# Sharing the last four evictions, waiting for the last stores ahead of a branch, and later branch hints

## The chip, the cores and the metric

The kernel runs on one core of a Trainium2 chip. The core has TensorE (PE, matrix products into PSUM), VectorE (DVE), ScalarE (ACT), GpSimd (POOL) and SyncE (SP, which mainly issues DMAs). The metric is the device time of one execution in microseconds (us); lower is better.

## The reference

Two attention blocks on inputs of 2048 rows and 512 columns, 32 heads of 16 columns each, in bfloat16. Block A is linear attention, block B full softmax attention; their outputs lie side by side in one output of 2048 x 1024:

```python
# A: phi(t) = where(t > 0, t + 1, exp(t)) + 1e-6
kv  = einsum("bhsd,bhse->bhde", phi(k), v);  z = sum of phi(k) over the rows
a   = (phi(q) @ kv) / (phi(q) . z + 1e-6)        # heads side by side, then @ A_wo
# B: scores = q k^T * 16**-0.5 for each head, 2048 x 2048
b   = softmax(scores) @ v                        # heads side by side, then @ B_wo
out = concatenate([a, b], axis=-1)
```

## The kernel before

Block B is the bulk: 32 heads with 2048 x 2048 scores each. It is cut into 32 units (4 groups of heads, 4 stretches of 512 query rows, 2 head parities). TensorE makes blocks of scores in PSUM; ScalarE takes the exponential of most of them (line 1111), and VectorE with GpSimd makes the rest by an integer approximation (lines 988 and 1184). TensorE then multiplies the results with V into `pPV` (line 1245). Block A, the projections and the output products fill the gaps.

The order of the work on each engine is not written by hand. When the program is built, a planner in Python runs a model of the engines: each job is a list of stages with an engine and an assumed duration; a stage becomes a candidate when the one before is over and visible, and the planner always takes the candidate that could start first, priorities breaking near ties. `go` adds an assumed extra delay `JM` (0.8 us) after a stage on GpSimd. What the planner emits is kept per engine in program order (`Sched.add`); semaphore waits follow from reads and writes.

The last unit is split in two halves of 256 query rows (`last_half`). Each half is transposed out of PSUM (line 1309), its row sums inverted (1310), multiplied (1311, the first half on GpSimd, the second on VectorE), and transposed into `ON` (1313). The output product has four parts for each of the last four tiles of 128 rows. Three need only earlier heads, and run ahead into free PSUM banks (`ahead_cand`); the fourth, in `last_tiles`, needs `ON`: tiles 0 and 1 the first half, tiles 2 and 3 the second. Each tile is then evicted from PSUM (the copy is at line 548) and stored (line 1333), 128 KB a store, by the SyncE queue or, for tile 3, by ScalarE's.

The integer approximation holds for a bounded range only. So the kernel tests the row sums: `bound_job` (lines 631 to 645), then `flag_job`, a small matrix product (652) and a reduction into `FLG` (653). At the end of its program each engine waits for the flag, loads it into a register (1606), and branches (1609): if the flag is set, it runs a second, general softmax program; if not, as with these inputs, it branches over that program to a drain and the end of the block (315). GpSimd alone waits for all stores ahead of its branch, in the operation named `final`.

The general program is thousands of instructions long on TensorE, ScalarE and VectorE, so the target of their branch is far from the code that runs ahead of it. The code comes in by DMA as the program runs (the queues of kind "instruction"). A `BRANCH_PREFETCH_HINT` (line 1608) names a branch to come as likely taken. `emit_queue` places it a given number of operations (`mark[0]`) ahead of the end of an engine's program; one operation of TensorE can be several matmuls.

Of the kernel before, what the change touches and what calls it, by code (L numbers as in the profile page):

```python
# [247 lines left out]
def bass_concat_heads__linear_attn_block__softmax_full_mha__prompt_kernel(nc, A_x, A_wqkv, A_wo, B_x, B_wqkv, B_wo, out):  # L248
# [39 lines left out]
    JM = 0.8  # L288
    DSH = 0.45
    XNT = 0.63  # L290
    VVT = 0.69
    HINT = 60
    HQ = ("pe", "act", "dve")
    FW = 3.4
    UT = 0.6
    AE = 40.0
# [18 lines left out]
    with es:  # L315
# [57 lines left out]
        def f32v(bk, n=512):  # L373
            return bk[0][:, bk[2]:bk[2] + n]
# [73 lines left out]
        for e_ in range(2):  # L448
            sch.add("dve", lambda e, e_=e_: e.tensor_reduce(PAR[:, e_:e_ + 1], ZMk[:].rearrange("p (a e) -> p e a", e=2)[:, e_, :],
                                                           axis=AX.X, op=ALU.max),  # L450
                    reads=["ZMk"], writes=[("PAR", e_)])
# [17 lines left out]
        def vis(eng, en_):  # L469
            return en_ + TAIL[eng] + SEM  # L470
# [3 lines left out]
        def lease(buf, readers):  # L474
            assert leases[buf] == 0, buf
            leases[buf] = readers
# [8 lines left out]
        def push(eng, ready, prio, dur, run, kind="f"):  # L485
            seq[0] += 1
            cands[eng].append((ready, prio, seq[0], dur, run, kind))

        class Job:
# [32 lines left out]
            def go(self, i, end, bk, bi):  # L522
                eng = self.stages[i][0]
                eng2, dur, fn = self.stages[i + 1]
                if getattr(fn, "buf", None) is not None:
                    lease(fn.buf, 1)
                push(eng2, end if eng2 == eng else vis(eng, end) + (JM if eng == "pool" else 0.0),
                     (CPRIO if i + 1 else self.prio) if eng2 == "pe" else (0 if eng2 == "act" or (i + 1 <= self.rel and self.bank) else min(self.prio, 2)), dur,
                     lambda st_, en_, fn=fn: (fn(bk), self.stage_done(i + 1, en_, bk, bi)), getattr(fn, "kind", "f"))

# [11 lines left out]
        def mm4(e, out, lhsT, rhs, start, stop):  # L542
            for g in range(4):
                ins = e.matmul(out[32 * g:32 * g + 32], lhsT=lhsT[:, 32 * g:32 * g + 32], rhs=rhs, start=start, stop=stop, tile_position=(0, 32 * g))  # L544
            return ins

        def copy_to(lane, out_fn, in_fn):
            return lambda e, bk: (e.tensor_copy(out_fn(), in_fn(bk)) if lane == "dve" else e.activation(out_fn(), in_fn(bk), ACTF.Copy))  # L548
# [248 lines left out]
        stores = []  # L797
        kst = lambda i: [("KV", i), ("KVV", i)]
# [45 lines left out]
        def unit(u):  # L844
            Gp, r2 = divmod(u, NC * 2)
            return (Gp,) + divmod(r2, 2)
# [63 lines left out]
        def cur_unit():  # L910
            for u in range(NU):
                if left[u]:
                    return u
            return None
# [374 lines left out]
            pr = 1 if out_ >= mode()[1] or final else 4  # L1289
            return [(t_, *make(rounds[:n]), pr) for n in range(len(rounds), 0, -1)]  # L1290

        FB = {}
        ahead = [(tl, hb) for tl in range(4) for hb in range(3)]

        def last_half(h, t_):

            if h == 0:
                lease("OT", 1)
            u, xb = LU, 0
            Gp, c, e_ = unit(u)  # L1300
            k = 4 * Gp + c
            o = OT[:, 0, :].rearrange("p (b r) -> p b r", r=32)
            xn = XN[:, xb, :].rearrange("p (b r) -> p b r", r=32)
            zs = ZRA[:, 16 * u + 8 * h:16 * u + 8 * h + 8]
            cs, bs = slice(256 * h, 256 * h + 256), slice(8 * h, 8 * h + 8)
            ot, zk, xk = [("OT", 0) if h == 0 else ("OT", 9)], [("ZR", u) if h == 0 else ("ZR", u + 9)], [("XN", xb, 1) if h == 0 else ("XN", xb, 9)]
            src, skey = (PVb, [("PV", g) for g in range(4)]) if h == 0 else (f32v(lbank[0]), [lbank[0][3]])
            mlane = "pool" if h == 0 else "dve"
            st = [("dve", 0.42, f_op("dve", lambda e: e.transpose(OT[:, 0, cs], src[:, 0:256]), skey, ot)),  # L1309
                  ("dve", 0.2, f_op("dve", lambda e: e.reciprocal(zs, o[:, bs, 16]), ot, zk)),  # L1310
                  (mlane, 0.44 if h == 0 else 0.27, f_op(mlane, lambda e: e.tensor_tensor(xn[:, bs, 16:32], o[:, bs, 0:16],
                                                                                  zs.unsqueeze(2).broadcast_to([128, 8, 16]), op=ALU.mult), ot + zk, xk)),
                  ("dve", 0.42, f_op("dve", lambda e: e.transpose(ON[:, k, cs], XN[:, xb, cs]), [("XN", xb, 0)] + xk, on_keys(k)[4 * h:4 * h + 4]))]
            urgent.append(Job(st, [("ot", u - 1)], [(3, ("onf", h))] + ([(1, ("zr", u))] if h else []), bank=False, ready=t_, prio=0.5))
            if h == 0:
                last_tiles()

        def last_tiles():

            Gp, c, e_ = unit(LU)  # L1320
            k = 4 * Gp + c
            for tl in range(4):
                def mm(bk, tl=tl):
                    bk = FB[tl]
                    sch.add("pe", lambda e: mm4(e, f32v(bk), ON[:, k, tl * 128:(tl + 1) * 128], WOb[:, 3, :], False, True),
                            reads=on_keys(k)[4 * (tl // 2):4 * (tl // 2) + 4] + [("Wb", 2)], writes=[bk[3]], accum=("ps", tl))
                mm.kind = "v"
                ln = ("act", "act", "dve", "act")[tl]
                def fin(bk, tl=tl, ln=ln):
                    bk = FB[tl]  # L1330
                    sch.add(ln, lambda e: copy_to(ln, lambda: obf(tl), lambda bk: f32v(bk))(e, bk), reads=[bk[3]], writes=kst(tl))
                    t = 4 * c + tl
                    stores.append(sch.add(out_lanes[tl], lambda e: e.dma_start(out[0][t * 128:(t + 1) * 128, 512:1024], obf(tl)),
                                          reads=kst(tl), queue="act" if tl == 3 else "sp", force_signal=True))
                urgent2.append(Job([("pe", 0.22, mm), (ln, 0.6 if ln == "dve" else 0.48, fin)], [("onf", tl // 2), ("ps", tl)] +
                                   [("akv", 1, bl) for bl in range(2)], [(-1, ("st", c, tl))], bank=False))

        def ahead_cand():
# [3 lines left out]
            if hb:  # L1342
                def more(st, en):
                    ahead.pop(0)
                    bk = FB[tl]
                    sch.add("pe", lambda e: mm4(e, f32v(bk), ON[:, 4 * hb + 3, tl * 128:(tl + 1) * 128], WOb[:, hb, :], False, False),
# [4 lines left out]
            fr = [(dfree[i], 0, ("d", i)) for i in range(len(dfree)) if dfree[i] is not None]  # L1351
            fr += [(afree[sl], 1, ("s", sl, b)) for sl in range(NS) if afree[sl] is not None for b in range(ABL[sl] - lent[sl]) if ("s", sl, b) not in FB]
            if not fr:
                return None
            t_, _, w_ = min(fr)
            def run(st, en):
                ahead.pop(0)
                FB[w_] = True
                if w_[0] == "d":
                    dfree[w_[1]] = None  # L1360
                    bk = DBANK[w_[1]]
                else:
                    bk = SBANKS[aoff[w_[1]] + w_[2]]
                FB[tl] = bk
                sch.add("pe", lambda e: mm4(e, f32v(bk), ON[:, 3, tl * 128:(tl + 1) * 128], WOb[:, 0, :], True, False),
# [144 lines left out]
        while True:  # L1510
# [42 lines left out]
            o = min((o for o in opts if o[0] <= t0 + 0.03), key=lambda o: (o[1], o[0], -o[3]))  # L1553
            st, _, eng, dur, run_, c_, kind = o
# [37 lines left out]
        sems = {ln: es.enter_context(nc.semaphore("s_" + ln)) for ln in sch.lane_ops.keys()}  # L1592
# [9 lines left out]
        def run(queue, e):  # L1602
            got, loc = [], []
            def hook(e):
                e.wait_ge(sems["dve"], flag_op.count)
                got.append(e.value_load(FLG.bitcast(mybir.dt.int32), min_val=0))
            sch.emit_queue(queue, e, sems, hook=(flag_op.idx if queue == "pool" else len(sch.ops), hook),
                           mark=(HINT, lambda e: loc.append(e.mark_branch_hint_location())) if queue in HQ else None)
            with e.If(got[0] > FLAG_BITS):
                if loc:  # L1610
                    bass.BassInstruction(list(loc[0].bb.instructions)[-1]).branch_hint(loc[0])
                for ln, tot in totals.items():
                    if tot:
                        e.wait_ge(sems[ln], tot)
                gsch.emit_queue(queue, e, gsems)
# [49 lines left out]
```

## Time and profile before

| | us |
|---|---|
| median of 3 runs | 678.11 (677.42 to 678.16) |
| the profiled execution | 678.51 |
| its span, first to last instruction | 676.8 |
| ScalarE busy | 659.0 (97%) |
| TensorE busy | 645.3 (95%) |
| VectorE busy | 593.4 (88%) |
| GpSimd busy | 590.5 (87%) |

The span is counted from the first instruction of the profiled execution to the last; the time of an execution has some more around it. In the rows below, "L1313" is line 1313 of the kernel, "out<-in" are the program's names of the tiles, "PEld" a weight load of TensorE, and a "q" behind an engine's name an instruction that its sequencer handles itself, such as issuing a DMA, a wait or a branch. Times in a timeline are start and length.

### The profile page before, as it was taken

To read this page: it belongs to the slowest core of one execution; us is meant where nothing else is said; L and a number is where in the kernel's file an instruction comes from. 1 tells how busy PE (TensorE), PEld (TensorE's weight loads), DVE (VectorE), ACT (ScalarE), POOL (GpSimd) and SP (SyncE) were. 2 spreads that over 40 slices of the span, in tenths; PEclk is the share of its full clock that TensorE was granted. 3 is DMA by queue.
4 is the path that set the end of the run, shared out by engine and by line. 5 is a ranking of instruction groups with operands and counts; after the bars stand their busy time and mean duration, and the time that the engine had idled before them with its cause. 6 is when DMAs were issued, how large, how long until landed. Compare 5 with 4: busy or idle time off the path is not lost.

```text
span 676.8 us, 19573 instructions
## 1 busy us (share of the span) xinstructions
PE 645.3 (95%) x8533; PEld 207.6 (31%) x8533; DVE 593.4 (88%) x973; ACT 659.0 (97%) x699; POOL 590.5 (87%) x369
## 2 busy tenths in 40 slices
PE   8999999999999999999999999999999999999996
PEld 4334322233333432222223333232222232222233
DVE  6987889988998999889898988989889898979993
ACT  5999999999999999999999999999999999999995
POOL 5699989998999898999999898898868999899893
PEclk9999999999999999999999999999989999999999
DMA  9401110111100021001011010211001000011001
GB/s 216 96 2 18 41 22 10 25 37 32 33 17 18 17 63 41 17 4 24 18 40 32 19 33 32 41 25 21 13 7 35 26 2 16 17 56 32 17 32 36
DMA packets 55418, 21.76 MB, mean 32 GB/s; under 512 B 45600, under 2 KB 55328, under 8 KB 55328
## 3 DMA queue, kind: packets, MB, share of 16 engines
q1 hardware_dynamic: 54128, 20.07, 13.2%
q8 instruction: 68, 1.11, 0.7%
q10 hardware_dynamic: 1200, 0.39, 0.2%
q14 instruction: 22, 0.18, 0.1%
HBM read 4.19 MB, written 4.19 MB: 12 GB/s over the span
## 4 chain that ended last, share of the span: by engine, by line
ACT 92%; PE 5%; DVE 1%; DMA 1%; issue 0%; ACTq 0%
ACT PT L1111 90%; ACT pD L701 2%; PE pS L881 2%; PE pPV L1245 1%; DMA xTb<-in_B_x_dram 1%; ACT pS L701 1%; PE pS L544 1%; PE pD L544 0%; PE pD L751 0%; PE pD L664 0%; DVE DI L988 0%; PE pS L573 0%; DVE OT L1309 0%; PE pD L573 0%; ACT KV L548 0%
## 5 line engine op out<-in xcount | busy, mean ns | idle before, releaser
L1111 ACT ACTIVATE PT<-pS 128x1024 f16<-128x1024 f32 (+1 forms) x659 | 649.2, 1326 | 4.1 <-PE pD L881 2.1
L1184 POOL TENSOR_SCALAR DJ<-DI 128x2048 int16<-128x2048 int16 x290 | 549.5, 1895 | 70.2 <-DVE DJ L1184 30.0
L988 DVE TENSOR_SCALAR DI<-pD 128x512 uint16<-128x512 f32 (+1 forms) x481 | 326.2, 695 | 36.5 <-PE pD L881 29.3
L881 PE MATMUL pS<-QT,KM 32*128 32x512 bf16 x1555 | 258.9, 385 | 20.8 <-ACT PT L1111 15.1
L1245 PE MATMUL pPV<-PT,VV 128*17 128x512 f16 (+1 forms) x1398 | 228.4, 379 | 0.0
L1245 PE MATMUL pPV<-DJ,VV 128*17 128x512 f16 (+1 forms) x1300 | 222.4, 379 | 0.0
L881 PE MATMUL pD<-QT,KM 32*128 32x512 bf16 x493 | 177.9, 385 | 0.2
L1245 PE MATMUL pPV<-DI,VV 128*17 128x512 f16 (+1 forms) x650 | 150.3, 380 | 0.7 <-DVE OT L1374 0.7
L881 PEld LDWEIGHTS pS<-QT,KM 32*128 32x128 bf16 x1555 | 64.3, 91 | 276.6 <-ACT PT L1111 238.3
L988 DVE TENSOR_SCALAR DI<-pS 128x512 uint16<-128x512 f32 x157 | 107.0, 681 | 3.8 <-PE pS L881 2.4
L1245 PEld LDWEIGHTS pPV<-DJ,VV 128*17 128x17 bf16 x1300 | 45.5, 88 | 44.1 <-issue 39.3
L1245 PEld LDWEIGHTS pPV<-PT,VV 128*17 128x17 bf16 x1398 | 46.3, 88 | 40.6 <-issue 35.9
L881 PEld LDWEIGHTS pD<-QT,KM 32*128 32x128 bf16 x493 | 42.0, 91 | 9.8 <-DVE DI L988 4.1
L1245 PEld LDWEIGHTS pPV<-DI,VV 128*17 128x17 bf16 x650 | 31.5, 88 | 23.3 <-issue 18.8
L1184 DVE TENSOR_SCALAR DJ<-DI 128x2048 int16<-128x2048 int16 x36 | 29.3, 815 | 0.0
L544 PE MATMUL pD<-Wa,xTa 128*32 128x256 bf16 x704 | 26.9, 274 | 0.3 <-DVE KV L702 0.3
L544 PE MATMUL pD<-xTb,Wb 128*32 128x512 bf16 x304 | 23.3, 383 | 0.0
L1374 DVE STREAM_TRANSPOSE OT<-pPV 128x512 f32<-128x512 f32 x31 | 21.9, 706 | 1.6 <-PE pPV L1245 1.6
L1379 POOL TENSOR_TENSOR XN<-OT,ZRA 128x256 bf16<-128x256 f32 x31 | 19.3, 622 | 3.6 <-DVE DJ L1184 2.5
L548 DVE CAST KV<-pD 128x512 bf16<-128x512 f32 x21 | 14.4, 686 | 5.8 <-PE pD L544 5.8
L701 ACT ACTIVATE pD<-pD 128x512 f32<-128x512 f32 x23 | 19.1, 829 | 0.3 <-DVE PQT L700 0.3
L544 PEld LDWEIGHTS pD<-Wa,xTa 128*32 128x32 bf16 x704 | 16.1, 96 | 9.6 <-issue 6.4
(117 smaller groups left out, 392.8 us busy)
## 6 DMA issues: line engine op xcount, KB each, us to landing
out_dram<-KV SPq DMA_DIRECT2D x31, 128.0 KB, 1.7
Wa<-in_A_wqkv_dram SPq DMA_DIRECT2D x3, 512.0 KB, 4.9
KM<-KR SPq DMA_DIRECT2D x96, 16.0 KB, 1.8
Wb<-in_B_wqkv_dram SPq DMA_DIRECT2D x2, 384.0 KB, 5.8
Wb<-in_B_wqkv_dram SPq DMA_DIRECT2D x1, 512.0 KB, 4.6
Wa<-in_A_wo_dram SPq DMA_DIRECT2D x1, 512.0 KB, 4.3
Wb<-in_B_wo_dram SPq DMA_DIRECT2D x1, 512.0 KB, 3.7
xTa<-in_A_x_dram SPq DMA_TRANSPOSE x24, 3.3
```

The costliest lines, as they stand in the source:

```text
L544: ins = e.matmul(out[32 * g:32 * g + 32], lhsT=lhsT[:, 32 * g:32 * g + 32], rhs=rhs, start=start, stop=stop, tile_position=(0, 32 * g))
L548: return lambda e, bk: (e.tensor_copy(out_fn(), in_fn(bk)) if lane == "dve" else e.activation(out_fn(), in_fn(bk), ACTF.Copy))
L701: ex = lambda bk: sch.add("act", lambda e: e.activation(x(bk), x(bk), ACTF.Exp), reads=[bk[3]], writes=[bk[3]])
L881: return e.matmul(dst, lhsT=KM[32 * g:32 * g + 32, Gp % 2, e_, j * 128:(j + 1) * 128], rhs=QT[32 * g:32 * g + 32, Gp % 2, c * 512:(c + 1) ...
L988: sch.add("dve", lambda e: e.tensor_scalar(DI.bitcast(U16)[:, buf, i * 512:(i + n) * 512], f32v(DBANK[bi], 512 * n), EB, IMAX, op0=ALU.add ...
L1111: sch.add("act", lambda e: e.activation(PT[:, row, c0:c0 + w], SCR[sl][:, 0:w], ACTF.Exp, scale=SC / ESC), reads=skeys(sl)[:len(bl)], writ ...
L1184: op = sch.add(ln, lambda e: e.tensor_scalar(J, I, 1.0, float(SH[k]), op0=ALU.mult, op1=ALU.add), reads=[("DI", buf, i) for i in range(n)] ...
L1245: sch.add("pe", lambda e: e.matmul(dst[32 * g:32 * g + 17, 0:n], lhsT=VV[:, Gp % 2, k, j, 17 * h:17 * h + 17], rhs=P[:, q0:q0 + n], start= ...
L1374: sch.add("dve", lambda e: e.transpose(OT[:, 0, :], PVb[:, 0:512]), reads=[("PV", g) for g in range(4)], writes=[("OT", 0)])
L1379: mul = f_op("pool" if XNP else "dve", lambda e: e.tensor_tensor(xn[:, :, 16 * e_:16 * e_ + 16], o[:, :, 0:16], zr.unsqueeze(2).broadcast_ ...
```

## The change

Four things change.

- In `go`, a stage that follows one on GpSimd is assumed ready 0.1 us after it, instead of 0.8 us, once all score blocks have been handed out (`cur_unit()` is None). This is in the last unit's tail alone.
- In `last_tiles`, tile 1 is evicted by VectorE instead of ScalarE, so that each engine has two of the four. The stores are listed in `fins` in the planner's order. A store goes by ScalarE's queue when ScalarE evicted the tile and two stores stand before it; all others go by SyncE's.
- Ahead of the branch, SyncE, TensorE, ScalarE and VectorE wait until the last two stores of `fins` have landed. The wait comes behind the load of the flag.
- The branch hint stands 8 operations ahead of the end on TensorE and VectorE, and 6 on ScalarE, instead of 60 on each.

```diff
-    HINT = 60
-    HQ = ("pe", "act", "dve")
+    HINT = {"pe": 8, "act": 6, "dve": 8}
...
-                push(eng2, end if eng2 == eng else vis(eng, end) + (JM if eng == "pool" else 0.0),
+                push(eng2, end if eng2 == eng else vis(eng, end) + (0.0 if eng != "pool" else JM if cur_unit() is not None else 0.1),
...
-        FB = {}
+        FB, fins = {}, []
...
-                ln = ("act", "act", "dve", "act")[tl]
+                ln = ("act", "dve", "dve", "act")[tl]
                 def fin(bk, tl=tl, ln=ln):
...
-                                          reads=kst(tl), queue="act" if tl == 3 else "sp", force_signal=True))
+                                          reads=kst(tl), queue="act" if ln == "act" and len(fins) >= 2 else "sp", force_signal=True))
+                    fins.append(stores[-1])
...
                 got.append(e.value_load(FLG.bitcast(mybir.dt.int32), min_val=0))
+                if queue != "pool":
+                    for o in fins[2:]:
+                        e.wait_ge(sems[o.lane], 16 * o.count)
             sch.emit_queue(queue, e, sems, hook=(flag_op.idx if queue == "pool" else len(sch.ops), hook),
-                           mark=(HINT, lambda e: loc.append(e.mark_branch_hint_location())) if queue in HQ else None)
+                           mark=(HINT[queue], lambda e: loc.append(e.mark_branch_hint_location())) if queue in HINT else None)
```

## The prediction

> **What bounds the kernel now.** I read the page first, then the chain of work that ended last from 660 us on, then the engines' timelines from 668 us on, and at last the rows of branches, hints and instruction packets. The page gives the whole span and the engines' shares of the chain:
>
> ```profile
> span 676.8 us, 19573 instructions
> ...
> ACT 92%; PE 5%; DVE 1%; DMA 1%; issue 0%; ACTq 0%
> ```
>
> ScalarE sets the time for 92% of the span, and the change touches none of that. It can move only what follows the last exponential, about 9 us. The chain's last piece, from its answer for 660 us on, is a ScalarE eviction:
>
> ```profile
> 672.09 0.18 ACT KV L548
> ```
>
> It ends at 672.27 us, 4.5 us ahead of the end of the span. What lies before it is in the timelines of VectorE, GpSimd, ScalarE and TensorE (start, length, instruction):
>
> ```profile
> 668.90 0.45 DVE L1313 STREAM_TRANSPOSE ON<-XN 128x256 bf16<-128x256 bf16 x1
> 669.27 0.20 DVE L631 TENSOR_REDUCE ZRA<-ZRA 128x1 f32<-128x17 f32 x2
> 669.43 0.15 DVE L644 TENSOR_SCALAR BN<-ZRA 128x1 f32<-128x1 f32 x1
> 669.62 0.16 DVE L645 SCALAR_TENSOR_TENSOR BN<-ZRA,BN 128x1 f32<-128x1 f32 x1
> 669.69 0.44 DVE L1313 STREAM_TRANSPOSE ON<-XN 128x256 bf16<-128x256 bf16 x1
> 670.06 0.65 DVE L548 CAST KV<-pS 128x512 bf16<-128x512 f32 x1
> 670.63 0.26 DVE L653 TENSOR_REDUCE FLG<-pPV 1x1 f32<-1x128 f32 x1
> ```
> ```profile
> 668.31 0.40 POOL L1311 TENSOR_TENSOR XN<-OT,ZRA 128x128 bf16<-128x128 f32 x1 [2.04 <-DVE ZRA L1310]
> ```
> ```profile
> 670.06 0.60 ACT L548 ACTIVATE KV<-pS 128x512 bf16<-128x512 f32 x1 [2.79 <-PE pS L544]
> 670.69 0.39 ACTq L1333 DMA_DIRECT2D out_dram<-KV  x1
> 671.18 0.60 ACT L548 ACTIVATE KV<-pD 128x512 bf16<-128x512 f32 x1 [0.52 <-PE pS L544]
> 671.68 0.59 ACT L548 ACTIVATE KV<-pS 128x512 bf16<-128x512 f32 x1
> ```
> ```profile
> 669.40 0.61 PE L544 MATMUL pS<-Wb,ON 128*32 128x512 bf16 x8 [0.23 <-DVE ZRA L631]
> 669.84 0.38 PE L652 MATMUL pPV<-BMk,BN 128*1 128x128 f32 x2
> 670.18 0.40 PE L544 MATMUL pD<-Wb,ON 128*32 128x512 bf16 x4
> 670.41 0.39 PE L544 MATMUL pS<-Wb,ON 128*32 128x512 bf16 x4
> ```
>
> The half that VectorE normalizes is transposed first (668.90), so tiles 2 and 3 come first. GpSimd's half is ready at 668.71 but is transposed only at 669.69, behind four small operations of the range test. Tiles 0 and 1 are then evicted by ScalarE one after the other, behind its store issue of 0.39 us.
>
> The rows of the output tensor say how long a store takes from issue to landing: the last one, then the first two, then all 32 of the run:
>
> ```profile
> L1333 SPq DMA_DIRECT2D out_dram<-KV x1: 332/332/332, 672.3 to 672.3; - x1
> ...
> DMA to landing us min/median/max: 4.0/4.0/4.0
> ```
> ```profile
> DMA to landing us min/median/max: 2.0/2.1/2.2
> ```
> ```profile
> DMA to landing us min/median/max: 1.7/1.7/4.2
> ```
>
> The last two stores take 4.2 and 4.0 us where the median is 1.7. The last lands at 672.3 + 4.0 = 676.3 and the span ends half a microsecond later: landing is what ends the kernel. Why it is slow, and what the change risks, is in the rows of the branch over the general softmax and of the drain behind it:
>
> ```profile
> L1609 DVEq COMPARE_BRANCH  x1: 84/84/84, 671.7 to 671.7; - x1
> L1609 PEldq COMPARE_BRANCH  x1: 409/409/409, 671.8 to 671.8; - x1
> L1609 ACTq COMPARE_BRANCH  x1: 68/68/68, 672.3 to 672.3; - x1
> ```
> ```profile
> L315 PEldq DRAIN  x1: 63/63/63, 672.3 to 672.3; - x1
> L315 ACTq DRAIN  x1: 81/81/81, 672.7 to 672.7; - x1
> L315 SPq DRAIN  x1: 13/13/13, 673.9 to 673.9; - x1
> L315 DVEq DRAIN  x1: 59/59/59, 675.1 to 675.1; - x1
> L315 POOLq DRAIN  x1: 50/50/50, 676.5 to 676.5; - x1
> ```
>
> From branch end to drain TensorE needs 0.1 us (672.2 to 672.3), ScalarE 0.4, but VectorE 3.4 (671.7 + 0.08 to 675.1). VectorE had nothing left to do: it was fetching the code behind the branch. It cost nothing, because GpSimd waited for the stores until 676.3. The hints were executed here:
>
> ```profile
> L1608 ACTq BRANCH_PREFETCH_HINT  x1: 55/55/55, 612.0 to 612.0; - x1
> L1608 DVEq BRANCH_PREFETCH_HINT  x1: 61/61/61, 628.1 to 628.1; - x1
> L1608 PEldq BRANCH_PREFETCH_HINT  x1: 45/45/45, 662.8 to 662.8; - x1
> ```
>
> And these are instruction packets, by stretches of the DMA view (packets, MB, share): from VectorE's hint to 666.6 us; 666.6 to 667; 667.8 to 668. TensorE's code comes on q8, the others' on q14:
>
> ```profile
> q1 hardware_dynamic: 720, 0.66, 5.0%
> q8 instruction: 4, 0.07, 0.7%
> ```
> ```profile
> q14 instruction: 1, 0.01, 6.6%
> ```
> ```profile
> q8 instruction: 1, 0.02, 29.1%
> ```
>
> Nothing came on q14 for 38 us after VectorE's hint: a hint does not fetch by itself. After TensorE's hint q8 brought one packet, in its steady pace (4 in 38.6 us above, so one in 9 or 10), and TensorE's branch then cost nothing. My reading is that a hint turns the next fetch of the running program to the branch's target, and that VectorE, whose hint stood in its last block, had no such fetch left.
>
> **The change part by part.** *GpSimd's result believed after 0.1 us instead of 0.8.* The planner then puts the second transpose right behind the first, at 669.27 instead of 669.69, with the four small operations behind it: 0.42 us earlier. TensorE is still busy with the first pair, which it takes at 0.23 us a tile, so the second pair starts at 669.40 + 2 x 0.23 = 669.86 instead of 670.18 (0.32 earlier) and ends near 670.25 and 670.48. The late ones now are the range test and the flag. With the test's last operation behind VectorE's second eviction the flag comes near 672.0 instead of 670.89; VectorE's branch came 0.8 us after the flag, so 672.8, which the wait for the stores (below, until 673.45) covers; a flag later than about 672.6 would cost its lateness one for one.
>
> *Evictions.* Tile 1 goes from ScalarE to VectorE. ScalarE: tile 3 at 670.06, tile 0 right behind it to about 671.2, with no store issue between. VectorE: tile 2 about 669.9 to 670.5, tile 1 about 670.6 to 671.3 (0.65 us each). The last eviction ends near 671.3 instead of 672.27: 1.0 us gained. The first two stores go through SyncE (0.33 us an issue), tile 0's from ScalarE when its work is over, tile 1's from SyncE at about 671.35; SyncE is free by then.
>
> *Waits for the last two stores.* SyncE, TensorE, ScalarE and VectorE wait with nothing queued behind but their branch and drain; GpSimd, which ends the kernel, waits for their drains. The gain: no code behind the branch is fetched while the stores fly. I price a store at 2.1 us, by the first two, which also flew as a pair; bounds are 1.7 (median) and 4.0 (no gain). Landing: 671.35 + 2.1 = 673.45, or 2.8 us earlier than 676.26. The cost: the branch can't start before 673.5, and what follows it is uncovered. A wait itself I take like a hint's row, 0.05 us.
>
> *Hints 8, 6 and 8 operations from the end.* Each hint is about 0.05 us and moves off a place where it cost nothing. VectorE's now comes at about 669.3, ScalarE's at 664.5, ahead of its packet at 666.6; TensorE's, ahead of the last three early matmul groups, near 668.3, behind its packet at 667.8. By my reading ScalarE keeps its fast branch, VectorE misses as it does now, and TensorE, which was fast, begins to miss. The price of a miss lies between 0.1 us (TensorE's row now: the hint works after all) and two of VectorE's stalls in a row, 6.8; I take VectorE's row, 3.4, for both, side by side, less 0.4 since no store packets are in the way any more: 3.0.
>
> *Sum.* Landing 673.45, wait and branch 0.1, TensorE's branch 0.41, miss 3.0, from the last drain to the end 0.3 (676.5 to 676.8): 677.3, against 676.8. So 2.8 us gained at the landing and 3.3 given back behind the branch: +0.5 us. The profiled execution took 678.51 us, 1.7 beyond its span, so 679.0; it lay 0.4 above the median of the runs, 678.11, so I predict 678.6. With 1.7 to 2.4 us for a store and 2.3 to 3.6 for the miss, this case alone spans 677.5 to 679.6.
>
> By the Trainium skill (Runtime: NRT & Kernel Launch, "Instruction fetch mechanics") prefetch is purely sequential, and a taken branch to a target outside the two blocks held always stalls for a fetch. TensorE's 0.1 us contradicts the "purely"; VectorE's 3.4 agrees. By that rule ScalarE would miss too, beside the others, and the sum would stay; and by it TensorE would have missed before, too.
>
> **The rivals.** *A late hint works (0.33).* If a hint within the last block fetches the target at once, all three branches are quick. Then 673.45 + 0.1 + 0.41 + 0.1 + 0.3 = 674.4, 2.4 us less: 675.7. For it: TensorE may have room for a third block where VectorE had none. Against it: VectorE had 43 us and got nothing. It needs both engines.
>
> *The two misses queue up (0.17).* TensorE and VectorE now ask for code at the same moment, where before their branches were fast or covered. If one fetch waits half a stall for the other, 1.7 us more: 680.3. It decides (more than 0.2% slower) from a stall of about 3.9 us on the last engine. For it: VectorE's single miss already took 3.4. Against it: q8 and q14 are separate queues.
>
> *The slow landing is not the code's (0.10).* If the last two stores take 4.0 us for another reason, landing is at 675.35, and the miss comes on top: 1.9 more, 680.5. Against it: the first two, from the same queues, landed in 2.0 and 2.2.
>
> **How the numbers follow.** 0.40 for my sum, at 678.6. Two runs of this kernel can be told apart from about 0.2%, 1.4 us: my sum is within that, so same is 0.40; faster is the working hint, 0.33; slower is the two others, 0.27. The range goes from the working hint with a 1.7 us store (675.2) to the queued miss (680.3).
>
> **What would show it.** Right: the second transposes back to back near 668.9 and 669.3; last eviction over by 671.4; all four stores landing in about 2 us, the last near 673.5; VectorE's drain some 3 us behind its branch, TensorE's too, and the span's end behind those drains and no longer behind a store. Wrong: drains within 0.5 us of the branches (then 675.7), a last store of 4 us with no instruction packets beside it, or a flag later than the landing.

## The result and the profile after

The changed kernel takes 679.30 us (median; 678.21 to 681.08) against 677.42 for the kernel before in the same series: a ratio of 1.0023, 95% interval 1.0013 to 1.0032. It is slower by about 0.2%.

The profiled execution has a span of 679.2 us, 2.4 more than before. 0.76 of that lies ahead of the change: the last exponential ends at 668.03 us instead of 667.27 (665.87 + 1.40 in the timeline of before). The first row below, the ScalarE timeline of the changed kernel, has this end; I count the tail from it. Before, the span ended 9.5 us behind it, now 11.2. The profiled execution took 681.08 us, the slowest of the eleven, so its span overstates the change; the tail's 1.7 us is close to the 1.9 us between the medians.

```profile
666.63 1.40 ACT L1030 ACTIVATE PT<-pS 128x512 f16<-128x512 f32 x2
670.82 0.60 ACT L547 ACTIVATE KV<-pS 128x512 bf16<-128x512 f32 x1 [2.79 <-PE pS L543]
671.32 0.59 ACT L547 ACTIVATE KV<-pD 128x512 bf16<-128x512 f32 x1
671.94 0.38 ACTq L1332 DMA_DIRECT2D out_dram<-KV  x1
```

VectorE's timeline of the same execution:

```profile
669.66 0.77 DVE L1312 STREAM_TRANSPOSE ON<-XN 128x256 bf16<-128x256 bf16 x2
670.35 0.21 DVE L630 TENSOR_REDUCE ZRA<-ZRA 128x1 f32<-128x17 f32 x2
670.61 0.69 DVE L547 CAST KV<-pS 128x512 bf16<-128x512 f32 x1
671.22 0.14 DVE L643 TENSOR_SCALAR BN<-ZRA 128x1 f32<-128x1 f32 x1
671.28 0.68 DVE L547 CAST KV<-pS 128x512 bf16<-128x512 f32 x1
671.88 0.15 DVE L644 SCALAR_TENSOR_TENSOR BN<-ZRA,BN 128x1 f32<-128x1 f32 x1
672.49 0.28 DVE L652 TENSOR_REDUCE FLG<-pPV 1x1 f32<-1x128 f32 x1 [0.47 <-PE pPV L651]
```

The two transposes now stand as one row, back to back. Both engines evict two tiles, and the last eviction is over at 671.96, 3.9 us behind the last exponential; before it was 5.0. So the compute part of the change did what it says. The stores of the same execution, by the rows of the output tensor (issue lengths as min/median/max):

```profile
L1332 SPq DMA_DIRECT2D out_dram<-KV x3: 332/492/1230, 671.3 to 673.0; - x3
L1332 ACTq DMA_DIRECT2D out_dram<-KV x1: 379/379/379, 671.9 to 671.9; - x1
...
DMA to landing us min/median/max: 1.9/2.3/2.7
```

No store takes 4 us any more. But SyncE's second issue took 1.23 us and pushed the last store to 673.0. It takes 0.42 us in most of the profiles below with the same evictions; with that, the last store would have started near 672.2. Then the branches, and the drains behind them:

```profile
L1612 DVEq COMPARE_BRANCH  x1: 84/84/84, 675.0 to 675.0; - x1
L1612 SPq COMPARE_BRANCH  x1: 58/58/58, 675.0 to 675.0; - x1
L1612 PEldq COMPARE_BRANCH  x1: 498/498/498, 675.0 to 675.0; - x1
```
```profile
L314 ACTq DRAIN  x1: 80/80/80, 675.4 to 675.4; - x1
L314 PEldq DRAIN  x1: 62/62/62, 675.6 to 675.6; - x1
L314 DVEq DRAIN  x1: 57/57/57, 678.9 to 678.9; - x1
```

All engines branch at 675.0, right behind the last landing. ScalarE and TensorE drain within 0.6 us; VectorE takes 3.9 us, and the span ends 0.3 us behind it. It was 3.4 us before, beside GpSimd's wait for the stores; now it stands at the end of everything. The hints, and one packet of the DMA view (671.6 to 671.7 us):

```profile
L1611 ACTq BRANCH_PREFETCH_HINT  x1: 55/55/55, 664.1 to 664.1; - x1
L1611 PEldq BRANCH_PREFETCH_HINT  x1: 45/45/45, 668.2 to 668.2; - x1
L1611 DVEq BRANCH_PREFETCH_HINT  x1: 56/56/56, 669.7 to 669.7; - x1
```
```profile
q8 instruction: 1, 0.02, 57.5%
```

This packet on TensorE's code queue has no counterpart before. It comes 3.5 us behind TensorE's late hint, and 0.1 us ahead of SyncE's long issue.

### The profile page after: what moved, and what is told of

Same layout as the page of the kernel before. It is cut to its first block, busy times and chain, and to the rows that moved or that the text cites. A ratio compares the mean times of both kernels' runs of the same rounds, so it can differ in the third digit from the quotient of the medians.

```text
span 679.2 us, 19577 instructions
## 1 busy us (share of the span) xinstructions
PE 645.7 (95%) x8533; PEld 208.1 (31%) x8533; DVE 593.8 (87%) x974; ACT 658.1 (97%) x698; POOL 589.9 (87%) x369
## 4 chain that ended last, share of the span: by engine, by line
ACT 92%; PE 5%; DVE 1%; DMA 1%; issue 0%
ACT PT L1110 90%; ACT pD L700 2%; PE pS L880 1%; PE pPV L1244 1%; DMA xTb<-in_B_x_dram 1%; ACT pS L700 1%; PE pS L543 1%; PE pD L543 0%; PE pD L750 0%; PE pD L663 0%; PE pS L572 0%; DVE DI L987 0%; PE pD L572 0%; DVE KV L547 0%; DVE OT L1308 0%
```

## The experiments

All ratios are against the kernel before on the same chip at the same time. "Behind the last exponential" is counted in each profile as above. Each edit is to the changed kernel unless it says otherwise.

**VectorE's hint alone, ahead of its last packet**

```diff
-    HINT = {"pe": 8, "act": 6, "dve": 8}
+    HINT = {"pe": 8, "act": 6, "dve": 120}
```

> The changed kernel with one number different: VectorE's branch hint stands 120 operations ahead of its end instead of 8, so ahead of the last instruction packet of its running program. Theory A (what ends the changed kernel is VectorE's code fetch of 3.9 us behind its branch, and a hint helps VectorE only when it stands ahead of that last packet): VectorE's drain comes within 0.5 us of its branch, the span ends about 0.3 us behind TensorE's drain, 3.3 us less than the changed kernel, about 676.0 us, 0.2% below the kernel before. Theory B (VectorE's hint does nothing wherever it stands, or the 3.9 us are no fetch): VectorE's drain still comes 3.9 us behind its branch, 679.3 us.

Ratio 1.0012 (0.9996 to 1.0028), median 678.6, with executions from 676.2 to 681.2. In the profile, of an execution of 679.0 us, VectorE's drain comes 0.5 us behind its branch, but TensorE's branch itself takes 3.78 us:

```profile
L1612 DVEq COMPARE_BRANCH  x1: 84/84/84, 673.1 to 673.1; - x1
L1612 SPq COMPARE_BRANCH  x1: 57/57/57, 673.1 to 673.1; - x1
L1612 PEldq COMPARE_BRANCH  x1: 3778/3778/3778, 673.1 to 673.1; - x1
```
```profile
L314 DVEq DRAIN  x1: 35/35/35, 673.7 to 673.7; - x1
L314 PEldq DRAIN  x1: 64/64/64, 677.0 to 677.0; - x1
```

So theory A holds for VectorE, and theory B falls. VectorE's hint now stands at 585.2 us, ahead of the last two packets on q14 before the branches (619.0 and 666.1 us); at 60 operations it stood between them (627.6 in the next experiment). The view doesn't say which engine a packet of q14 is for; that the one at 619.0 is VectorE's last is my inference. The time did not follow, because in this profile TensorE missed. Its late hint, the same as in the changed kernel, brought no packet of its own here. The hint, and a packet on q8 that starts between 666.9 and 667.0 us, right behind it:

```profile
L1611 PEldq BRANCH_PREFETCH_HINT  x1: 45/45/45, 666.9 to 666.9; - x1
```
```profile
q8 instruction: 1, 0.02, 60.8%
```

**The hints back to 60**

```diff
-    HINT = {"pe": 8, "act": 6, "dve": 8}
+    HINT = {"pe": 60, "act": 60, "dve": 60}
```

> The changed kernel with the three hints back at 60 operations ahead of the end; evictions and waits stay. Theory A: VectorE misses as before (3.4 to 3.9 us from branch to drain), TensorE and ScalarE stay quick, so about the time of the changed kernel, 678.5 to 679.5 us; the instruction packet that TensorE's late hint brought at 671.6 us is gone, and if it was what held SyncE's second store issue for 1.23 us, that issue takes 0.33 again and the last store lands 0.7 us earlier. Theory C (the late hints are what costs the change its gain): back below the kernel before, about 676 us.

Ratio 1.0011 (1.0001 to 1.0020), 678.39 us. TensorE and ScalarE are quick, VectorE takes 3.6 us (branch at 673.1, drain at 676.7). No packet comes beside the stores, the longest issue is 0.45 us instead of 1.23, and the stores land in 1.7 to 2.1 us:

```profile
L1332 SPq DMA_DIRECT2D out_dram<-KV x3: 332/424/446, 670.0 to 670.9; - x3
L1332 ACTq DMA_DIRECT2D out_dram<-KV x1: 378/378/378, 670.6 to 670.6; - x1
...
DMA to landing us min/median/max: 1.7/1.9/2.1
```
```profile
L314 DVEq DRAIN  x1: 58/58/58, 676.7 to 676.7; - x1
```

The late hints are therefore not the main loss (theory C falls). They may make it larger: the tail is 10.3 us here against 11.2. But that is one profile each, and the intervals of the two ratios overlap.

**No waits for the stores**

```diff
-                if queue != "pool":
-                    for o in fins[2:]:
-                        e.wait_ge(sems[o.lane], 16 * o.count)
```

> The changed kernel without the waits for the last two stores; evictions and late hints stay. Theory A (the waits put VectorE's fetch behind the landing instead of beside it): VectorE branches about 1.4 us earlier, its drain comes 3.4 to 3.9 us later near 677.3 us of the span, the last stores take up to 4 us again beside instruction packets; the later of the two ends the span: about 677.5 us, 1.5 to 2 us below the changed kernel and near the kernel before. Theory D (the waits protect the stores and gain what they were priced at, the loss is elsewhere): slower than the changed kernel.

Ratio 1.0011 (1.0002 to 1.0021), 678.1 us: near theory A's time, and not slower than the changed kernel, as it would be by theory D. TensorE missed again, 4.02 us in its branch, and its drain came last, where theory A had VectorE's:

```profile
L1609 PEldq COMPARE_BRANCH  x1: 4022/4022/4022, 672.1 to 672.1; - x1
```
```profile
L314 DVEq DRAIN  x1: 58/58/58, 675.3 to 675.3; - x1
L314 PEldq DRAIN  x1: 64/64/64, 676.2 to 676.2; - x1
```

Another part of the expectation was wrong: the stores landed in 1.7 to 2.1 us without the waits, the last one 6.3 us behind the last exponential. They are over before the packets behind the branches come (the first at 6.8 us). Two things put them ahead. The last store is issued 0.9 us earlier than in the kernel before, and the flag comes 1.1 us later, so that TensorE and VectorE branch at 5.9 us instead of 4.5 and 4.4. In the kernel before, the first packet behind the branches came at 5.9 us, when a store that lands at 6.3 is still in flight. So the later flag has a part in it; no run separates the two.

**The kernel before with the waits alone**

```diff
@@ kernel before: stores listed in fins, its own evictions and hints
+                if queue != "pool":
+                    for o in fins[2:]:
+                        e.wait_ge(sems[o.lane], 16 * o.count)
```

> The kernel before plus only the waits for the two stores that come last in its plan; its evictions, order and hints (60) stay. Theory A: the last store, issued 5.0 us behind the end of the last exponential, lands in about 2 us instead of 4.0, then VectorE's 3.4 to 3.9 us follow: 1.5 to 2 us above the kernel before, about 679.2 us. Theory D: the landing 2 us earlier is a gain, about 675.5 us.

Ratio 1.0021 (1.0010 to 1.0032), 678.92 us. The waits do protect the stores: the last two, 4.2 and 4.0 us in the kernel before, take 1.7 each, and landing is 2.3 us earlier in the tail. Then VectorE takes its 3.0 us (branch at 675.1, drain at 678.2), and the end is 0.8 us later than before. What the wait gains at the landing is given back behind the branch, as theory A expected.

```profile
DMA to landing us min/median/max: 1.7/1.9/2.2
```
```profile
L315 DVEq DRAIN  x1: 58/58/58, 678.2 to 678.2; - x1
```

**Order and evictions alone** (no waits, all hints at 60)

```diff
-    HINT = {"pe": 8, "act": 6, "dve": 8}
+    HINT = {"pe": 60, "act": 60, "dve": 60}
...
-                if queue != "pool":
-                    for o in fins[2:]:
-                        e.wait_ge(sems[o.lane], 16 * o.count)
```

> The changed kernel with neither the waits nor the late hints (60 operations on all three): what is left is the order of the two transposes and the shared evictions. Theory A: evictions over and stores landed as in the changed kernel (6.3 us behind the last exponential), but VectorE, whose flag comes 1.1 us later than in the kernel before, branches at 5.9 us and pays its 3.2 to 3.4 us of fetch: end near 9.5 us, the kernel before's, 677.5 us. Rival E (the shared evictions gain what they were priced at, 1.0 us or more): 676.5 us or less.

Ratio 1.0005 (0.9996 to 1.0014): no difference. Stores landed at 6.3 us, 2.7 us earlier than before; VectorE's drain, at 9.1 us, took over the end (9.4, before 9.5). That is theory A's end; rival E falls.

```profile
L314 DVEq DRAIN  x1: 58/58/58, 675.5 to 675.5; - x1
```

**All hints ahead of the last packets, with the waits**

```diff
-    HINT = {"pe": 8, "act": 6, "dve": 8}
+    HINT = {"pe": 60, "act": 60, "dve": 120}
```

> The changed kernel with all three hints ahead of the last instruction packet of their engine: 60 operations from the end on TensorE and ScalarE, 120 on VectorE. Theory A (the fetches behind the branches of VectorE and, with its late hint, in some executions of TensorE, are all that the waits uncover): all drains within 0.6 us of their branches, last store about 6.3 us behind the last exponential's end, span's end 7.2 to 7.3 us behind it instead of 9.5 (kernel before) and 11.2 (changed kernel): 2.2 us below the kernel before, 675.3 us. Theory B (some engine always pays a fetch): the end stays 10 us or more behind the last exponential, 678 us or more.

Ratio 0.9973 (0.9963 to 0.9983), 675.81 us: 1.8 us below the kernel before, where theory A had 2.2, and theory B falls. Landing at 6.3, both late drains within 0.6 us, end at 7.3 us behind the last exponential:

```profile
L314 PEldq DRAIN  x1: 63/63/63, 675.2 to 675.2; - x1
L314 DVEq DRAIN  x1: 36/36/36, 675.2 to 675.2; - x1
```

**The same without the waits**

```diff
-    HINT = {"pe": 8, "act": 6, "dve": 8}
+    HINT = {"pe": 60, "act": 60, "dve": 120}
...
-                if queue != "pool":
-                    for o in fins[2:]:
-                        e.wait_ge(sems[o.lane], 16 * o.count)
```

> The same with the early hints, but without the waits for the last two stores; evictions stay. Theory A (with every branch hinted in time the only packets left are those that follow a taken branch; the stores, issued 0.9 us earlier than in the kernel before, are landed or nearly so when these come): last store lands 6.3 us behind the last exponential, GpSimd's branch follows it at once, end at 6.8 us: 2.7 us below the kernel before, 674.8 us, and 0.4 below the version with waits, since TensorE's branch of 0.4 to 0.5 us is taken beside the landing. Rival D (the waits are needed to protect the stores): the last store takes 4 us again, end near 8.7 us, 0.8 below the kernel before.

Ratio 0.9964 (0.9952 to 0.9977), 674.93 us. The stores land at 6.3 us as with the waits (1.7 to 2.1 us each), all drains are done within 0.3 us of it, and the end is at 6.8 us. It is faster than both the kernel before and the changed kernel. One of its six executions took 676.99 us; it was not profiled, and its cause is open. Rival D falls: with this order and these evictions the waits protect nothing. The stores and the drains:

```profile
L1332 SPq DMA_DIRECT2D out_dram<-KV x3: 332/423/442, 669.6 to 670.4; - x3
...
DMA to landing us min/median/max: 1.7/1.9/2.1
```
```profile
L314 POOLq DRAIN  x1: 50/50/50, 672.8 to 672.8; - x1
L314 DVEq DRAIN  x1: 39/39/39, 672.8 to 672.8; - x1
L314 PEldq DRAIN  x1: 11/11/11, 672.8 to 672.8; - x1
```

**The kernel before with VectorE's hint alone moved**

```diff
-                           mark=(HINT, lambda e: loc.append(e.mark_branch_hint_location())) if queue in HQ else None)
+                           mark=(120 if queue == "dve" else HINT, lambda e: loc.append(e.mark_branch_hint_location())) if queue in HQ else None)
```

> The kernel before with VectorE's hint 120 operations from the end instead of 60, and nothing else. Theory A: VectorE's drain within 0.6 us of its branch, which alone is worth nothing, since the stores end the kernel. If VectorE's fetch was what held up the last two stores (4.2 and 4.0 us), they land in about 2 us and the kernel gains up to 2 us, 675.5 us; if other engines' packets did it, they still take 4 us and the time stays 677.5 us.

Ratio 0.9992 (0.9983 to 1.0002): no difference. VectorE is quick (branch at 671.1, drain at 671.7), yet the last two stores still take 3.7 and 3.4 us. While they fly, between 672 and 674 us, these came:

```profile
q1 hardware_dynamic: 269, 0.25, 38.2%
q14 instruction: 3, 0.02, 5.2%
q8 instruction: 1, 0.02, 4.5%
```

So, by one profile of each, VectorE's fetch is at most the small part of the disturbance (0.4 to 0.5 us a store); packets come behind the other branches as well, hinted or not.

**TensorE's late hint alone, in the fastest version**

```diff
-    HINT = {"pe": 60, "act": 60, "dve": 120}
+    HINT = {"pe": 8, "act": 60, "dve": 120}
```

> The fastest version so far (shared evictions, no waits, VectorE's hint at 120, ScalarE's at 60) with TensorE's hint alone moved from 60 operations to 8 ahead of the end, behind the packet that brings its last block. Theory F (a late hint of TensorE leads to a packet of its own in some executions and to none in others): executions of two kinds, near 674.9 us where the packet comes and near 678 us where TensorE's branch takes 3.8 to 4.0 us instead of 0.5. Theory G (TensorE always has room, and its two long branches in earlier runs came from something else): 674.9 us in all. Theory H (it never works by itself): 678 us in all.

Ratio 0.9992 (0.9978 to 1.0006); the executions are of two kinds: three from 675.2 to 675.6 us, nine from 677.4 to 679.4. That is as theory F has it, and theories G and H fall; that the nine are executions with a long branch was not seen, since none of them was profiled. The profile is of the quick kind: a packet on q8 3.2 us behind the hint, a branch of 0.64 us, and again one long SyncE issue. The hint stands here right behind a packet on q8 that starts at 666.0 us:

```profile
L1608 PEldq BRANCH_PREFETCH_HINT  x1: 45/45/45, 666.1 to 666.1; - x1
```
```profile
L1332 SPq DMA_DIRECT2D out_dram<-KV x3: 333/427/1442, 669.2 to 671.1; - x3
```

**The old evictions with the waits and VectorE's early hint** (from the kernel before)

```diff
@@ kernel before: stores listed in fins
+                if queue != "pool":
+                    for o in fins[2:]:
+                        e.wait_ge(sems[o.lane], 16 * o.count)
...
-                           mark=(HINT, lambda e: loc.append(e.mark_branch_hint_location())) if queue in HQ else None)
+                           mark=(120 if queue == "dve" else HINT, lambda e: loc.append(e.mark_branch_hint_location())) if queue in HQ else None)
```

> The kernel before, its old evictions and order, with the waits for its last two stores and VectorE's hint at 120: the version with all hints early and waits, less the shared evictions and the order of the transposes. Theory A: last store landed 6.7 us behind the last exponential instead of 6.3, so the end 7.7 us behind it instead of 7.26: 1.8 us below the kernel before, about 675.9 us; the 1.0 us by which the evictions are over earlier is worth 0.5. Rival E (evictions worth their full 1.0 us): 676.6 to 676.9 us.

Ratio 0.9964 (0.9952 to 0.9976), 676.21 us. In the profile the last store lands at 6.7 us and the end is at 7.7, 0.5 behind the version with shared evictions and waits. The times can't separate the two: their intervals overlap, and the kernel before was slower in this series (678.22 us, against 677.76 in the other), which lowers this ratio. By the profiles the shared evictions and the order are worth 0.5 us here, as theory A expected.

## Why the prediction was right, and where it was not

The forecast was a gain at the landing given back behind the branch, for a net of +0.5 us within a range of 675.2 to 680.3. Both halves happened; the measured loss is larger, 1.9 us, and with 0.23% just beyond the 0.2% I had set for "same". That 678.6 lies within 0.7 us of the measured 679.30 is in part luck: I had added 0.5 to 678.11, and the kernel before took 677.42 in the series of the result. Counted from the last exponential, my sum put the end at 10.0 us, and the profiled execution ended at 11.2. The landing was 0.7 later and VectorE's miss 0.9 longer than in the sum. Against them stand 0.4 us for TensorE's branch, which the sum put ahead of the miss: VectorE, whose miss ends the kernel, does not wait for it.

- *Transposes, second pair, evictions, flag.* Right, each within 0.1 us counted from the last exponential (last eviction 3.9 us behind it, predicted 4.0; flag's end 4.75, predicted 4.7).
- *Price of a store, 2.1 us.* Right: 1.7 to 2.2 where no packet is in the way, and 1.9 for the last store of the changed kernel. The term ahead of it was mis-sized: "SyncE is free by then" left out an issue of 1.23 us, which put the landing 0.7 us later than forecast in the profiled execution.
- *The gain, put to the waits.* This step failed. The shared evictions, the order and the later flag bring the stores in ahead of the packets without them; the waits are worth 2.3 us at the landing only with the old evictions. In the changed kernel they only move VectorE's fetch back: with the hints at 60, the end is at 10.3 us with the waits and at 9.4 without.
- *VectorE misses, ScalarE does not.* Right, and the reason is borne out: VectorE's hint at 8 or 60 operations gave 3.0 to 3.9 us from branch to drain in each profile, at 120 it gave 0.5. ScalarE's hint at 6 operations stood 3.3 us ahead of a packet on q14, and its drain came 0.4 us behind its branch. I took 0.4 off the 3.4 because no store would be in the way; in the changed kernel it was 3.9, so that correction had the wrong sign there. The other misses, 3.0 to 3.6, do not separate with the waits from those without.
- *TensorE begins to miss.* Half right. I read the hint as turning the next regular packet, and put the late hint 0.5 us behind the start of the last one. It came 0.9 us earlier than I had it, within 0.5 us of that start on either side. In two profiles (the changed kernel, and TensorE's late hint alone) the packet had started 0.13 us ahead of the hint; the hint brought a packet of its own 3.5 and 3.2 us later, and the branch was quick. In the two others (VectorE's hint alone, and no waits) the packet started 0.06 and 0.49 us behind the hint; no packet of its own came, and the branch took 3.8 and 4.0 us. With the hint at 60 operations, the next packet starts 4.5 to 5.1 us behind it in each profile, and the branch is quick. So a hint just ahead of a packet looks lost and one just behind it does not, the reverse of my reading. Four profiles suggest this, and no run was made to test it. In the version that changes only this hint, nine of twelve executions were of the slow kind.
- *Rivals.* The working late hint failed on VectorE, which alone decides. Two misses at once (the version without waits) took 3.2 us on VectorE and 4.0 on TensorE, against 3.0 to 3.9 and 3.8 where each missed alone, so neither waited half a stall for the other. The third rival's time, 680.5, lay outside the range I gave. The slow landing does go with the branches: held back by the waits, the same two stores with the old evictions took 1.7 us each.

The Trainium skill's rule (Runtime: NRT & Kernel Launch, "Instruction fetch mechanics") that a taken branch outside the held blocks stalls for a fetch agrees with the 3.0 to 4.0 us; that prefetch is purely sequential does not, since with hints in time all three branches are through in 0.4 to 0.6 us.

## What to carry to other kernels

A wait that protects one transfer also delays what stands behind it: before adding it, look for work that was late but covered, here a code fetch of 3.4 us beside a landing. Place a branch hint well ahead of the last instruction packet of each engine's running program, engine by engine: here 3.3 us or more ahead worked, and 0.5 us or less, in two profiles, did not. Read the branch's length and the distance to the drain to see whether it worked. Once the last stores land ahead of what follows the branches by themselves, the wait for them is only a cost.

## What the runs showed of the hardware

A miss of TensorE shows inside the branch (3.8 and 4.0 us instead of 0.4 to 0.6), a miss of VectorE between branch and drain. Both profiles in which a packet of TensorE's code fell on the stores' issue have one long SyncE issue (1.23 and 1.44 us), and none of the others has (0.33 to 0.45); that the packet causes it was not shown by itself. The last two stores of the kernel before, with the packets behind the branches beside them, took 4.2 and 4.0 us, and 3.7 and 3.4 with VectorE's early hint. With TensorE's one packet beside their issue stores took 1.8 to 2.9 us, and without packets 1.7 to 2.2. That the packets slow them, and not something else that follows a branch, was not shown by itself.
